# GeGLU block on one core: the plain halves of eight tile pairs first, and M1 held in the memory of h

## The chip, the core and the metric

One of the eight cores of a Trainium2 chip runs the whole program. Its engines work side by side, each in the order of its own instruction stream: TensorE (PE in the profile, with its weight loads as PEld) multiplies matrices into eight banks of accumulator memory of 128 x 512 f32; VectorE (DVE), ScalarE (ACT) and GpSimd (POOL) do the elementwise work; SyncE (SP) issues transfers, and ACT issues some too. The metric is the device time of one launch in microseconds. The median of three runs was 539.03 us before the change (538.69 to 539.42).

## The reference

```python
def reference(x, w_gate, w_up, w_down):
    return (_gelu(x @ w_gate) * (x @ w_up)) @ w_down
```

x is 2,048 tokens by 1,024 (D), the gate and up weights are 1,024 by 3,584 (F), the down weights 3,584 by 1,024, all bf16; gelu is the tanh form. Call h the product of gelu and up, 2,048 by 3,584.

## The kernel before

**Halves and blocks.** The tokens are worked in two halves of 1,024; in each, h is made whole (gate and up) and then multiplied by the down weights. A half has two token blocks of 512 (tb 0 and 1). F is cut into 28 tiles of 128 columns, seven chunks of four tiles; a pair is two tiles. D is cut into eight slices of 128, that is two K halves of four slices.

**Seven products for eight.** For a pair of tiles, two token blocks and two K halves, the plain way takes eight block products of four matmuls each, for gate and again for up: 64 matmuls. The kernel uses a Strassen-Winograd scheme of seven products, 56 matmuls. M1 and M2 are plain (bf16: tile 0 of the pair by block 0, first and second K half), and their sum is tile 0 on block 0. The five others (M5, M6, M7, M3, M4, in this order) multiply sums: s1 to s4 and a copy a22 of the weight blocks of the pair, and t1 to t4 and a copy b22 of the token blocks. The sums are stored as f32r (four bytes) in `s_mem` and `t_mem`, so these are the f32 matmuls of the profile. The t sums are made once per half, by DVE (b22 by ACT). The s sums are made for every pair, eight by POOL (s1, s2, s3, s4 for gate and up, index j) and two copies by ACT; there is one buffer for each, so POOL may overwrite s1 for the next pair once M5 has read it, and so on.

**One group.** `quads` (L406) works two pairs at a time in the eight banks, which are named in twos (one for gate, one for up): PB, VB, QB, RB. M1 goes to a first bank and ACT copies it to Q (L444); M2 is added to the first bank, which ACT (gelu) and DVE (multiply, L291) turn into a tile of h. Then for each pair: M5 into V, copied to memory m by ACT (L472); M6 added to Q, copied to R by ACT (L478); DVE adds m to Q (L434); M7 added to R, DVE writes R + m to V, which gives tile 1 on block 1; M3 added to Q gives tile 0 on block 1; M4 added to R gives tile 1 on block 0. Functions in a dictionary (`thens`) are called at named points between these steps; they place other work in the streams.

**The start.** The first pair of the first half is not done by the scheme: `first_pair_units` (L329) computes it plainly on both blocks, 64 bf16 matmuls (L267), while x and the weights arrive, and the t sums are made (`t_sum`, L241). The first x slices are transposed by TensorE (`transpose_x0`, L302), the others by transposing transfers on SP. Pair 1 then runs alone through `quads`, with sums made early: M5 twice ahead of M6 there, and one quarter of t4 on POOL. Six groups of two pairs follow. In the gaps of these groups DVE makes sums of the down weights, stored to a scratch tensor in device memory (`stage_step`, L614: 42 steps, each a DVE operation, most with a store); `run_steps(n)` places the next n of them, `run_loads` the loads ahead of them and `run_x` transposing transfers of the second half's x.

**Order.** Every helper `pe`, `act`, `dve`, `pool`, `sp` ties an instruction behind the previous one of its engine (`on`, L110): each stream is exactly the order in which the kernel's code calls them. An instruction that waits holds all that stand behind it on its engine. Eight transfer semaphores are used in turn, and a transfer is issued only when the transfer eight places earlier has landed.

**Memory.** The weights of two chunks are held in `w_mem` (`new_chunk`, L146), by even and odd chunk number; hT, 28 rows of 1,024 tokens, is h of one half, with a row for each tile.

Of the kernel before, what the change touches and what calls it, by code (L numbers as in the profile page):

```python
# [10 lines left out]
BF16 = mybir.dt.bfloat16  # L11
# [23 lines left out]
def kernel(  # L35
# [8 lines left out]
    nc = tc.nc  # L44
# [97 lines left out]

    xs0 = w_mem[:, 4 * CH : 4 * CH + TSB * D].rearrange("p (a b) -> p a b", b=D)
    chunks = {}

    def new_chunk(key):  # L146
        c0 = 2 * CH * (key[1] % 2)
        chunks[key] = tuple(
            w_mem[:, c0 + j * CH : c0 + (j + 1) * CH].rearrange(
                "p (a b) -> p a b", b=FG  # L150
            )
            for j in range(2)
        )
# [33 lines left out]
    load_x0(0, sp, 0, 2)  # L187
    load_x0(0, act, 2, TSB)
    load_w(first, 0, 0, 2, sp, 0, FA)
    load_x0(1, act)  # L190
    load_w(first, 1, 0, 2, sp, 0, FA)
    load_w(first, 0, 2, 5, act, 0, FA)
    load_w(first, 1, 2, 5, sp, 0, FA)
# [20 lines left out]
    load_xT(xT, 0, 0, KH, KH + 1)  # L214
    behind_transpose = last_on["sp"]
    load_xT(xT, 0, 0, KH + 1, KH + 2)
    for j in range(2):
        load_w(first, j, 5, KD, act, 0, FA)
        tc.add_manual_dep(
            last_on["act"].ins,  # L220
            behind_transpose.ins.name,
            SCHED_DEP,
            reason="engine order",
        )
    act(nc.scalar.preload_act_table(ACT.Gelu_apprx_tanh))
    load_xT(xT, 0, 0, KH + 2, KD)
    for k0, k1 in ((0, 2), (2, KH), (KH, KD)):
        load_xT(xT, 0, 1, k0, k1)
    for j in range(2):
        load_w(first, j, 0, KD, sp, FA, FG)  # L230
    new_chunk((0, 1))
    for j in range(2):
        load_w((0, 1), j, 0, KD)
# [31 lines left out]
    def mm_gu(ps, w_sb, fi, tb, kd):  # L265
        pe(
            nc.tensor.matmul(  # L267
                ps[:],
                lhsT=w_sb[:, kd, fi * P : (fi + 1) * P],
                rhs=xT[tb][:, kd, :],  # L270
                start=(kd == 0),
                stop=(kd == KD - 1),
            )
        )

# [23 lines left out]
    def unit_out(hT, bset, fi, tb):  # L299
        mult(hT, gelu(banks[bset[0]]), banks[bset[1]], fi, tb)  # L300

    def transpose_x0(q):  # L302

        parts = [(2 * q, 0, 4), (2 * q + 1, 0, 4)]
        if q == 0:
            parts = [(0, 0, 2), (0, 2, 4), (1, 0, 4)]
        for n, (kd, ts0, ts1) in enumerate(parts):
            tp = banks[(PB + QB)[(2 * q + n) % 4]][:].bitcast(BF16)
# [14 lines left out]
    def part(held, tb, k0, k1, us=(0, 1), js=(0, 1)):  # L323
        for kd in range(k0, k1):
            for j in js:
                for u in us:
                    mm_gu(banks[held[u][j]], chunks[first][j], u, tb, kd)

    def first_pair_units(hT):  # L329

        held = (VB, RB)
        transpose_x0(0)
        warm(RB[1], TB // 2)
        part(held, 0, 0, KPQ, js=(0,))
        transpose_x0(1)
        part(held, 0, 0, KPQ, js=(1,))
        part(held, 0, KPQ, KD)
        t_sum("t1", 0, KH // 2)
        t_sum("t1", KH // 2, KH)
        for u in range(2):  # L340
            unit_out(hT, held[u], u, 0)
        held = (QB, PB)
        part(held, 1, 0, KH)
        t_sum("t2")
        t_sum("b22")
        t_sum("t3", 0, KH // 2)
        part(held, 1, KH, KD, (0,))
        unit_out(hT, held[0], 0, 1)
        t_sum("t3", KH // 2, KH)
        part(held, 1, KH, KD, (1,))  # L350
        unit_out(hT, held[1], 1, 1)
        for j in range(2):
            s_sum(0, 1, j, "s3", True, False)
        for name in ("s1", "s2", "s4"):
            for j in range(2):
                s_sum(0, 1, j, name)
# [5 lines left out]
    def block(key, j, i, kh):  # L362
        fi = 2 * (key[2] % PPG) + i
# [704 lines left out]
```

## Time and profile before

| | |
|---|---|
| median of three runs | 539.03 us |
| span of the profiled execution | 537.4 us (its own time lies with the runs, 538.69 to 539.42) |
| TensorE busy | 533.6 us, 2,388 matmuls recorded |
| DVE, ACT, POOL busy | 367.6, 263.5, 252.2 us |
| first plain product (L267) | 4.98 us |
| first product of `quads` | 19.66 us |
| first f32 product | 22.93 us |
| gate and up of the first half end | 182.87 us |
| granted TensorE clock, mean | 1.000 |

How to read it: matmuls are pipelined, so their recorded lengths overlap and the rate is read from starts, or from the length of a run of them. In a timeline a row gives start, length, engine, line, operation, output <- inputs, shapes and how many instructions were merged; in square brackets stands the idle time ahead of it and what ended that. Lengths of DVE and POOL rows overlap by some 0.04 to 0.09 us.

### The profile page before, as it was taken

The page shows a single profiled execution, that of the slowest core. Times are in us where ns is not written, and L with a number is a line of the kernel's source. Part 1 is how long each engine was busy: PE and PEld are TensorE (multiplying, and loading weights), DVE is VectorE, ACT ScalarE, POOL GpSimd, SP SyncE. Part 2 cuts the span into 40 slices and gives each one's busy share as a digit, 9 for nine tenths or more (in the row PEclk, how much of TensorE's full clock was granted, in tenths as well). Part 3 has the DMA queues.
Part 4 walks back from the last instruction along what each step waited for, and adds up shares of the span by engine and source line. Part 5 has one row for each costly group of instructions (what it writes and reads, how often), then busy time and mean ns, then how long its engine had stood idle before and what let it go on. Part 6 is the DMA issues. An engine that isn't in the chain of part 4 may idle for free.

```text
span 537.4 us, 7033 instructions
## 1 busy us (share of the span) xinstructions
PE 533.6 (99%) x2388; PEld 379.2 (71%) x2388; DVE 367.6 (68%) x476; ACT 263.5 (49%) x447; POOL 252.2 (47%) x213
## 2 busy tenths in 40 slices
PE   9999999999999999999999999999999999999997
PEld 4568686867677686777768676776768686866866
DVE  2985868787876998989555353444444669979961
ACT  2555555556465329117465554656555551452280
POOL 0698696969696200000056494958677670000000
PEclk9999999999999999999999999999999999999999
DMA  9965759697623887788950413314040329677846
GB/s 220 329 199 134 267 164 304 182 320 199 229 53 143 318 288 243 243 292 292 329 168 12 145 62 97 110 48 154 3 156 22 136 84 337 228 237 250 292 143 212
DMA packets 92547, 102.70 MB, mean 191 GB/s; under 512 B 18656, under 2 KB 67424, under 8 KB 92512
## 3 DMA queue, kind: packets, MB, share of 16 engines
q1 hardware_dynamic: 69568, 80.23, 45.7%
q10 hardware_dynamic: 22944, 22.02, 13.2%
q8 instruction: 19, 0.31, 0.3%
q14 instruction: 16, 0.13, 0.1%
HBM read 85.98 MB, written 12.58 MB: 183 GB/s over the span
## 4 chain that ended last, share of the span: by engine, by line
PE 99%; ACT 0%; issue 0%
PE bank L418 63%; PE bank L698 33%; PE bank L267 3%; PE bank L202 1%; PE bank L311 0%; ACT o_sb L754 0%
## 5 line engine op out<-in xcount | busy, mean ns | idle before, releaser
L418 PE MATMUL bank<-t_mem,s_mem 128*128 128x512 f32 x1056 | 244.6, 392 | 0.0
L418 PEld LDWEIGHTS bank<-t_mem,s_mem 128*128 128x128 f32 x1056 | 198.1, 188 | 42.7 <-issue 0.2
L388 POOL TENSOR_TENSOR s_mem<-w_mem 128x512 fp32r<-128x512 bf16 x102 | 124.0, 1236 | 185.5 <-DMA out_dram<-o_sb 96.9
L698 PE MATMUL bank<-t_mem,s_mem 128*128 128x512 f32 (+1 forms) x548 | 127.2, 391 | 0.0
L698 PEld LDWEIGHTS bank<-t_mem,s_mem 128*128 128x128 f32 x548 | 102.5, 188 | 22.0
L291 DVE TENSOR_TENSOR hT<-w_mem,bank 128x512 bf16<-128x512 f32 x106 | 72.5, 687 | 66.5 <-PE bank L418 44.5
L434 DVE TENSOR_TENSOR bank<-bank,m 128x512 f32<-128x512 f32 x108 | 70.0, 694 | 56.1 <-ACT m L472 54.3
L418 PE MATMUL bank<-xT,w_mem 128*128 128x512 bf16 x432 | 95.7, 379 | 0.0
L286 ACT ACTIVATE w_mem<-bank 128x512 f32<-128x512 f32 x106 | 63.0, 597 | 64.1 <-DVE bank L434 34.8
L418 PEld LDWEIGHTS <-w_mem 128*128 128x128 bf16 x432 | 41.2, 98 | 51.3 <-issue 3.4
L388 POOL TENSOR_TENSOR s_mem<-w_mem,s_mem 128x512 fp32r<-128x512 bf16 x52 | 68.4, 1335 | 2.9 <-PE bank L418 2.9
L600 DVE TENSOR_TENSOR t_mem<-w_mem 128x1024 fp32r<-128x1024 bf16 x56 | 65.9, 1225 | 0.9 <-PE bank L418 0.9
L388 POOL TENSOR_TENSOR s_mem<-s_mem,w_mem 128x512 fp32r<-128x512 f32 x52 | 61.3, 1200 | 0.0
L401 ACT CAST s_mem<-w_mem 128x512 fp32r<-128x512 bf16 x54 | 33.2, 616 | 31.3 <-PE bank L418 30.1
L478 ACT COPY bank<-bank 128x512 f32<-128x512 f32 x54 | 30.8, 570 | 26.6 <-PE bank L418 26.6
L670 DVE TENSOR_TENSOR s_mem<-hT 128x512 fp32r<-128x512 bf16 x52 | 36.7, 745 | 7.1 <-PE bank L698 7.1
L472 ACT COPY m<-bank 128x512 f32<-128x512 f32 x54 | 31.8, 589 | 18.4 <-PE bank L418 18.4
L698 PEld LDWEIGHTS <-hT 128*128 128x128 bf16 x224 | 21.3, 98 | 26.6 <-issue 2.1
L444 ACT COPY bank<-bank 128x512 f32<-128x512 f32 x54 | 30.7, 570 | 14.3 <-PE bank L418 13.5
L625 DVE TENSOR_TENSOR o_sb<-wd_sb,o_sb 128x512 fp32r<-128x512 bf16 x28 | 32.9, 1176 | 0.5
L763 ACT CAST o_sb<-bank 128x512 bf16<-128x512 f32 x27 | 14.8, 585 | 33.8 <-PE bank L698 33.8
L597 ACT CAST t_mem<-w_mem 128x1024 fp32r<-128x1024 bf16 x28 | 26.9, 1047 | 0.0
(46 smaller groups left out, 236.5 us busy)
## 6 DMA issues: line engine op xcount, KB each, us to landing
t_mem<-t_dram SPq DMA_DIRECT2D x56, 512.0 KB, 5.3
w_mem<-in_w_gate_dram ACTq DMA_DIRECT2D x10, 1024.0 KB, 5.4
w_mem<-in_w_up_dram ACTq DMA_DIRECT2D x10, 1024.0 KB, 8.3
wd_sb<-in_w_down_dram SPq DMA_DIRECT2D x28, 256.0 KB, 5.4
t_dram<-o_sb SPq DMA_DIRECT2D x28, 256.0 KB, 3.5
wd_sb<-in_w_down_dram SPq DMA_DIRECT2D x12, 512.0 KB, 7.6
w_mem<-in_w_down_dram SPq DMA_DIRECT2D x4, 1024.0 KB, 6.7
w_mem<-in_w_down_dram SPq DMA_DIRECT2D x8, 512.0 KB, 8.3
```

What stands on the lines that cost most here:

```text
L286: act(nc.scalar.activation(out=g_sb, in_=ps[:], func=ACT.Gelu_apprx_tanh))
L291: nc.vector.tensor_tensor(out=hT[:, fc, tb * TB : (tb + 1) * TB], in0=g_sb, in1=ps[:], op=ALU.mult,)
L388: pool(nc.gpsimd.tensor_tensor(out=t, in0=in0, in1=in1, op=op))
L401: act(nc.scalar.copy(out=t, in_=a(1, 1)))
L418: nc.tensor.matmul(banks[bank][:], lhsT=lhs[:, c, :], rhs=rhs[:, c, :], start=start and c == 0, stop=c == KH - 1, skip_group_check=True,)
L434: nc.vector.tensor_tensor(out=banks[dst][:], in0=banks[src][:], in1=m5[:], op=ALU.add)
L472: act(nc.scalar.copy(out=m5[j][:], in_=banks[V_[j]][:]))
L478: act(nc.scalar.copy(out=banks[R_[j]][:], in_=banks[Q_[j]][:]))
L600: dve(nc.vector.tensor_tensor(out=t, in0=in0, in1=in1, op=ALU.subtract))
L625: dve(nc.vector.tensor_tensor(out=t, in0=in0, in1=in1, op=ALU.subtract))
L670: dve(nc.vector.tensor_tensor(out=t, in0=in0, in1=in1, op=op))
L698: nc.tensor.matmul(banks[bank][:, c0:c1], lhsT=lhs(i, u), rhs=rhs(i)[:, c0:c1], start=start and i == 0, stop=stop and i == NS - 1, skip_gr ...
```

## The change

- The first half's pairs are formed anew: the first eight pairs are tile p with tile p + 8 (p from 0 to 7), the other six pairs two neighbours as before.
- `first_units` takes the place of `first_pair_units`: it computes tiles 0 to 7 on block 0 alone, plainly, two tiles at a time with gate and up in four banks, two such sets in the eight banks. That is M1 (slices 0 to 3) and M2 (slices 4 to 7) of the eight pairs. Between the two K halves ACT copies M1 of each tile, for gate and for up, as f32 into rows of hT that are not yet written (`p_hold`, `hold`).
- Then `quads` runs with all eight pairs and `plain=False`: no M1 and M2, only the five sums' products of each pair; ACT fetches the held M1 into Q ahead of each pair. In this run s3 of gate is made by DVE, the others by POOL, and M5 stands ahead of M6 in each pair.
- t4 is made by DVE whole; its quarter on POOL is gone. In the stream of DVE t1 stands behind the multiplies of the first two sets, t2 and t3 behind those of the third, then the multiplies of the fourth.
- Loads: x and chunk 0 in other pieces and with the x transposes of four slices in one transfer; chunk 0 (and later chunk 3) lies in hT; chunks 1 and 2 are loaded at the start on SP, chunk 1 ahead of the second block's x, chunk 2 behind it. Chunk 3 is loaded by ACT in two halves, at the start of pairs 1 and 3, chunks 4 and 5 at pairs 4 and 7. The staging loads are moved behind the start.
- One staging step stands at the start and at M3 of pairs 1 to 7; then three groups of two pairs follow, each with four steps at M1, three at the start of the sums, and one at M3 and one at M4 of each pair.

The core of the diff:

```diff
+    NL = 8
+    LEAD = tuple((p, p + NL) for p in range(NL))
+    HF = 2 * NL
+    HELD = ((0, 0), (0, 3))
...
+    def p_hold(pair, j):
+        if j == 1 and pair % 2 == 1:
+            return hT0[:, pair - 1 : pair + 1, TB:SH].bitcast(F32)
+        f = NL + pair if j == 0 else KF - 4 + pair // 2
+        m = hT0[:, f : f + 1, :].rearrange("p a (b c) -> p (a b) c", b=2)
+        return m.bitcast(F32)
...
-    load_xT(xT, 0, 0, KH + 2, KD)
-    for k0, k1 in ((0, 2), (2, KH), (KH, KD)):
+    load_xT(xT, 0, 0, KH, KD)
+    for f0 in (FA, 0):
+        for j in range(2):
+            load_w(first, j, KH, KD, sp, f0, f0 + FA)
+    new_chunk((0, 1))
+    for k0, k1 in ((0, KH), (KH, KD)):
+        for j in range(2):
+            load_w((0, 1), j, k0, k1)
+    for k0, k1 in ((0, KH), (KH, KD)):
         load_xT(xT, 0, 1, k0, k1)
-    for j in range(2):
-        load_w(first, j, 0, KD, sp, FA, FG)
-    new_chunk((0, 1))
-    for j in range(2):
-        load_w((0, 1), j, 0, KD)
+    new_chunk((0, 2))
+    for f0 in (0, FA):
+        for j in range(2):
+            load_w((0, 2), j, 0, KD, sp, f0, f0 + FA)
...
+    def hold(held, tiles, j):
+        for u, t in enumerate(tiles):
+            act(nc.scalar.copy(out=p_hold(t, j), in_=bank2(held[u][j])))
...
+        outs(*rest(1))
+        outs(*rest(0))
+        for j in range(2):
+            top(2, j, 0, KH)
+        for j in range(2):
+            top(3, j, 0, KH)
         t_sum("t1", 0, KH // 2)
         t_sum("t1", KH // 2, KH)
...
+        outs(*rest(2))
         t_sum("t2")
+        t_sum("t3", 0, KH // 2)
+        t_sum("t3", KH // 2, KH)
         t_sum("b22")
...
+        outs(*rest(3))
+        for name in ("s3", "s1", "s2", "s4"):
             for j in range(2):
-                s_sum(0, 1, j, name)
+                s_sum(0, 0, j, name)
...
-    def quads(hT, h, members, nxt, thens, m5_first):
+    def quads(hT, h, members, nxt, thens, m5_first, plain=True):
...
+        def fetch(n):
+            for j in range(2):
+                act(nc.scalar.copy(out=bank2(run[n][4][j]), in_=p_hold(n, j)))
...
+                    dve_too = not plain and (name, j) == ("s3", 0)
+                    s_sum(after[0], after[1], j, name, dve_too, False)
...
+            if not plain and n + 1 < len(run):
+                fetch(n + 1)
...
+            thens[0]["start"] = [
+                lambda j=j: s_sum(0, 0, j, "a22") for j in range(2)
+            ] + [lambda: t_sum("t4", 0, KH // 2)]
+            thens[0]["m5"] = [lambda: t_sum("t4", KH // 2, KH - 1)]
+            thens[0]["v of gate"] = [lambda: t_sum("t4", KH - 1, KH)]
+            for n in range(1, len(LEAD)):
+                thens[n]["start"] = [lambda: run_steps(1), run_loads]
+                thens[n]["m3"] = [lambda: run_steps(1), run_loads]
...
+            thens[1]["start"].append(lambda: load_half(0))
+            thens[3]["start"].append(lambda: load_half(FA))
+            thens[4]["start"].append(lambda: load_chunk((0, 4)))
+            thens[7]["m7"] = [lambda: load_chunk((0, 5))]
+            quads(hT, h, range(len(LEAD)), (h, begin), thens, True, False)
...
-                few = lead == begin
-                add(0, "m1", lambda n=3 if few else 4: run_steps(n))
-                add(0, "start", lambda n=1 if few else 3: run_steps(n))
+                add(0, "m1", lambda: run_steps(4))
+                add(0, "start", lambda: run_steps(3))
...
+                    add(n, "m4", lambda: run_steps(1))
```

## The prediction

> **What bounds the kernel now.** I read the page's busy shares first, then the chain that ended last in order of time, then the timeline of TensorE, and last the timelines of DVE and POOL in the first 40 us, where the change is made.
>
> ```profile
> span 537.4 us, 7033 instructions
> PE 533.6 (99%) x2388; PEld 379.2 (71%) x2388; DVE 367.6 (68%) x476; ACT 263.5 (49%) x447; POOL 252.2 (47%) x213
> PE bank L418 63%; PE bank L698 33%; PE bank L267 3%; PE bank L202 1%; PE bank L311 0%; ACT o_sb L754 0%
> ```
>
> ```profile
> 4.98 1.44 PE bank L267 x4
> ...
> 6.87 12.95 PE bank L267 x60
> 19.82 163.21 PE bank L418 x728
> ```
>
> ```profile
> 39.02 18.51 PE L418 MATMUL bank<-t_mem,s_mem 128*128 128x512 f32 x80
> 57.37 7.08 PE L418 MATMUL bank<-xT,w_mem 128*128 128x512 bf16 x32
> 64.10 18.51 PE L418 MATMUL bank<-t_mem,s_mem 128*128 128x512 f32 x80
> 82.45 7.08 PE L418 MATMUL bank<-xT,w_mem 128*128 128x512 bf16 x32
> ```
>
> ```profile
> 15.24 2.29 DVE L262 TENSOR_TENSOR t_mem<-xT,t_mem 128x2048 fp32r<-128x2048 bf16 x1
> 17.45 2.18 DVE L262 TENSOR_TENSOR t_mem<-xT 128x1024 fp32r<-128x1024 bf16 x1
> ...
> 20.14 1.58 DVE L262 TENSOR_TENSOR t_mem<-xT 128x1024 fp32r<-128x1024 bf16 x1
> 21.64 0.68 DVE L291 TENSOR_TENSOR hT<-w_mem,bank 128x512 bf16<-128x512 f32 x1
> 22.24 2.62 DVE L386 TENSOR_TENSOR s_mem<-w_mem 128x512 fp32r<-128x512 bf16 x2
> ...
> 25.39 1.60 DVE L262 TENSOR_TENSOR t_mem<-xT,t_mem 128x1024 fp32r<-128x1024 bf16 x1
> 26.91 1.95 DVE L434 TENSOR_TENSOR bank<-bank,m 128x512 f32<-128x512 f32 x3
> 28.77 0.93 DVE L262 TENSOR_TENSOR t_mem<-xT,t_mem 128x512 fp32r<-128x512 bf16 x1
> 29.62 0.69 DVE L434 TENSOR_TENSOR bank<-bank,m 128x512 f32<-128x512 f32 x1
> ```
>
> ```profile
> 20.60 3.72 POOL L388 TENSOR_TENSOR s_mem<-s_mem,w_mem 128x512 fp32r<-128x512 f32 x2
> 24.27 3.74 POOL L388 TENSOR_TENSOR s_mem<-w_mem,s_mem 128x512 fp32r<-128x512 bf16 x2
> 27.97 1.17 POOL L260 TENSOR_TENSOR t_mem<-xT,t_mem 128x512 fp32r<-128x512 bf16 x1
> 29.83 2.29 POOL L388 TENSOR_TENSOR s_mem<-w_mem 128x512 fp32r<-128x512 bf16 x2 [0.68 <-PE bank L418]
> ```
>
> TensorE is the chain from 0.77 us to the end and waits for next to nothing. So a matmul less is time won, and any wait that reaches TensorE is time lost. A plain bf16 matmul costs 12.95/60 = 0.216 us. A group of two pairs takes 82.45 - 57.37 = 25.08 us for 32 bf16 and 80 f32 matmuls, so an f32 one costs (25.08 - 32 x 0.216)/80 = 0.227 us, and four of them 0.91 us. The DVE lines are the pass in which the block sums are made for the first pair of sums; the next-to-last block shows that this pass, from t2's start to the add that frees the gate-and-up bank (29.62 + 0.69), lasts 15.06 us with no idle. The POOL lines show one operation at 1.13 to 1.17 us alone, and 1.6 to 2.1 us where DVE runs an operation on memory beside it; DVE's own are stretched too (a half of t3 is 2.18 and 1.58 here, against 1.22 for the same size at 11.64).
>
> **Part 1: matmuls.** The trace has 720 plain bf16 and 1,644 f32 matmuls (80 of the bf16 ones ahead of the first sum); the instructions of the changed program, as built, hold 48 fewer bf16 and 40 more f32: the first pair is no longer computed plainly on both blocks. 48 x 0.216 - 40 x 0.227 = 10.4 - 9.1: **-1.3 us**, all on the path. No row says that these matmuls could have another pace, so both ends are -1.3.
>
> **Part 2: the sums of the token blocks now stand behind the plain halves, with no cover after them.** The first f32 matmul was due at 23.12 (19.66 plus 16 x 0.216) and is due 48 x 0.216 later: 33.5. Call t = 33.5 the start of the sums. Their ten products take 0.91 us each: M5 twice, M6 twice, M7 from t + 3.6, M3 from t + 5.4, M4 from t + 7.3; the last product, M4 of up, is due at 41.6. Before, 3.5 us of plain products stood between the block sums and M5, and the pass began 8 us ahead of it.
> After, DVE's order puts t2 behind the two multiplies of the third set, whose last product ends 16 plain matmuls ahead of t, at 30.0. The multiplies start 0.60 apart (rows of that kind), so t2 starts at 31.2. Until M4 of up, DVE has: t2, t3 in halves, two multiplies, t4's first half, two adds, a quarter of t4, an add, another quarter of t4 (POOL's before), s3 of the next pair (POOL's for most pairs before), an add. All wait only for DVE itself.
> - Lowest: every operation at its undisturbed start-to-start time, 2.2 + 1.26 + 1.15 + 0.6 + 0.6 + 1.15 + 0.6 x 4 + 0.72 + 0.6 + 0.7 = 11.4 us: ready at 42.6, 1.0 us late.
> - Nearest row: the pass shown above, 15.06 us from t2 to the same add. The new one has a multiply (0.65) and an s3 (1.31) less and a quarter of t4 (0.93) more: 14.0 us, ready at 45.2, 3.6 late. But in that pass t2 ran undisturbed at 2.29; POOL is now busy with the first pair's sums in that time, so I add 0.5 (the mean stretch of the six disturbed rows: 0.95, 0.36, 0.36, 0.97, 0.37, 0.25).
> - Highest: each of the seven memory operations waits for most of a POOL operation (0.95, the largest stretch): 11.4 + 6.6 = 18, ready at 49.2, 7.6 late.
> I take **+4.2 us**, by the nearest row. On the way M7 of up waits for a bank that the second of those multiplies holds, M3 for the adds into its banks, M4 for t4's last quarter; these fall inside the 4.2. A rule speaks against the change here. The Trainium skill, SBUF — State Buffer, "two separate sides", says that DVE operations with two inputs in memory and GpSimd operations exclude each other for the whole instruction. The trace agrees in the main: at 34.9 us two such DVE operations take 1.53 us each and POOL's 1.6, against 0.68 and 1.13 alone, nearly the two in turn. By the rule in full the stall would be the upper end, 7.6, and the sum 546.4; by the nearest row it is 543.0.
>
> **Part 3: what must be there by then.** For pair 0 POOL makes eight sums from the weights of chunks 0 and 2; the last piece it needs is behind about 7.0 MB. In the five stretches of 5 us from the start the trace moved 171, 257, 226, 322 and 355 GB/s, and 244 in the next: 7.0 MB at some 26.5 us. Five operations of 1.13 from there bring s2 of up to 32.2; it is due at 36.2. POOL's cover is 4 us; without it each late us is a us. Cost **0** (0 to 2). The second block's transposes pass SP behind chunk 1's loads, about 6 MB: due in front of t1, which has until 33.
>
> **Part 4: the start.** Weights of four tiles, not two, are wanted from 5 us; the first eight loads carry 1.0 MB, as before 1.15. One transpose of four blocks replaces three; a like one landed 4.4 us after its issue at 10.32 (ACT waited for it until 14.8), so issued near 5 it is there at 10, due at 12.8. The weights behind it (rows of 4.6 to 5.7 us to landing, issued at about 7.3) come at 12 to 13. Holding M1 costs 16 copies from a bank on ACT; no row has one into this memory, but the copies to m are 0.59 and from bank to bank 0.57. The fourth pair of copies frees its bank about 0.1 us after it is wanted. **+0.3** (0 to 1.0; a gain is excluded, TensorE had no idle there).
>
> **Part 5: the eight pairs.** 40 x 0.227 = 9.1 us each. POOL has seven sums, 7 x 1.13, and three DVE operations that stretch it by 0.47: 9.3. It falls 0.2 us back in a pair, 1.6 in seven; the sums are finished about 6 us ahead of their use, so **0** (0 to 3, if each stretch is 0.68 or more). DVE has seven bank operations at 0.61 and three others at about 1.2: 7.9. ACT has eleven of 0.57 to 0.62, 6.5, with M1 fetched from memory instead of copied between banks: 0. The loads of chunk 3 now stand on ACT ahead of the M5 copies of pairs 1 and 3, and wait for POOL's last sum that reads the old weights; with two issues (0.4 and 0.5 in the rows) the copies come 1 to 2 us late, of which M7 forgives 0.3 to 1. **+0.4** (0 to 1.8). The other moved issues on SP (staging loads, their stores, next block's x) have a pair's time each: 0.
>
> **Part 6: the staged sums** of the down weights start a pair later and run 11 instead of 9 to a group. In the group at 82.45 DVE is free 0.7 us before the first add; one step more (0.68 to 1.5) fits in front of the multiplies, except in the last group, where two more sums stand there: **+0.4** (0 to 1).
>
> **Sum.** -1.3 + 4.2 + 0 + 0.3 + 0.4 + 0.4 = +4.0. The profiled execution spans 537.4 us; the median of the runs is 539.03, 1.6 us of which lie around the span, so it stands with the other runs. 539.0 + 4.0 = **543.0 us**.
>
> **Rivals.**
> - *The gain is kept.* If DVE has add and s3 behind it at 41.6, the saved matmuls remain: 539.0 - 1.3 = 537.7. It decides if t2 starts before 30.2. For it: every transfer has landed by then and DVE is idle from about 24 us. Against it: the order, in which t2 stands behind those multiplies. Chance 0.06.
> - *Undisturbed DVE:* 539.0 - 1.3 + 1.0 and up to 1.3 from parts 4 to 6: 538.7 to 540.0, about no change (0.2%, 1.1 us, is what a measurement here can tell). Against it: POOL is seldom idle from 27 us on. 0.08.
> - *POOL becomes the bound* of the eight pairs: at 0.9 per stretch, 10.6 us a pair against 9.1, 10.5 in seven less the 6 of lead: about 4.5 more, 547.5. 0.10.
> - *Late weights of chunk 2* (2 us): 545. 0.07.
> - *TensorE's clock falls.* The first matmuls take 0.43 us until 5.8 us, then 0.216. If the gaps in pair 0 bring that back for 3 us, 1.5 us more: 544.5. The Trainium skill, TensorE: Matmul & The Clock Gate, Part 1, asks for an idle window of 3.4 us; my gaps are 2 us at most. 0.03.
> - That the change leaves the matmuls in is excluded by the count in part 1.
>
> **Numbers.** My forecast has 0.66 and runs from 540.5 to 546. Low end of the range 539.7 (cuts off the kept gain and most of the undisturbed case), high end 547 (leaves out most of POOL's). Faster 0.06, same 0.08, slower 0.86.
>
> **What the profile would show.** Right: TensorE at 0.216 to about 33.5 us, then gaps in the first 40 f32 matmuls alone that sum to some 4 us, their releasers DVE (adds, t4) and ACT's copy to the R banks; t2 starting at 31 to 32 us; pairs 2 and 4 to 7 at 9.1 us. Wrong: t2 running before the multiplies, DVE ahead of M4, or TensorE waiting for POOL or for transfers; and then the sum is off by the term of that part.

## The result and the profile after

| | before | after |
|---|---|---|
| median of the runs | 539.1 us (538.69 to 539.42) | 551.74 us (550.42 to 553.68) |
| ratio after to before | | 1.0239, interval 1.0215 to 1.0262 |
| span of the profiled execution | 537.4 us | 549.4 us (its own time 551.18) |
| first f32 product starts | 22.93 us | 36.38 us |
| granted TensorE clock, mean | 1.000 | 0.992 |

The kernel became 12.7 us slower. The forecast was 543.0 us, and its range ended at 547.0: the sign was right and the size was a third of what came. The page after, with its busy times and the chain by engine:

```profile
span 549.4 us, 7112 instructions
PE 536.3 (98%) x2359; PEld 382.6 (70%) x2380; DVE 370.9 (68%) x487; ACT 274.1 (50%) x471; POOL 259.8 (47%) x214
PE 86%; DMA 5%; SPq 4%; DVE 3%; POOL 1%; issue 1%; ACT 0%; ACTq 0%; DVEq 0%; POOLq 0%
```

TensorE was nearly the whole chain before; now 5% of it are transfers, 4% the issues of SP and 3% DVE. The timeline of TensorE tells where (in brackets the idle time ahead of a run of matmuls and what ended it):

```profile
19.32 13.98 PE L337 MATMUL bank<-xT,w_mem 128*128 128x512 bf16 x62
36.38 11.75 PE L470 MATMUL bank<-t_mem,s_mem 128*128 128x512 f32 x36 [3.08 <-POOL s_mem L438]
49.38 4.85 PE L470 MATMUL bank<-t_mem,s_mem 128*128 128x512 f32 x20 [1.26 <-DVE bank L486]
55.71 60.87 PE L470 MATMUL bank<-t_mem,s_mem 128*128 128x512 f32 x264 [1.48 <-ACT bank L531]
...
123.15 18.51 PE L470 MATMUL bank<-t_mem,s_mem 128*128 128x512 f32 x80
...
155.45 12.94 PE L470 MATMUL bank<-t_mem,s_mem 128*128 128x512 f32 x56 [1.40 <-DVE bank L486]
...
190.45 3.89 PE L470 MATMUL bank<-t_mem,s_mem 128*128 128x512 f32 x16 [0.61 <-DVE bank L486]
```

There are five waits: one in front of the first product of sums (for POOL), one in front of M4 of up of pair 0 (49.38, for DVE), one in pair 1 (55.71, for ACT), and two in the groups of two pairs. The first 16 f32 matmuls show something else. Where nothing else holds them their starts lie 0.427 us apart, not 0.227, and the granted clock says the same. The columns are busy time and count of PE, PEld, DVE, ACT and POOL, then the granted clock, the share of the transfer engines and GB/s:

```profile
35.00:40.00 5.00, 3.60 (x8) 2.40 (x9) 5.00 (x5) 0.59 (x1) 5.00 (x4) 0.60 0.44 160
40.00:45.00 5.00, 5.00 (x17) 3.80 (x16) 2.14 (x4) 1.73 (x3) 5.00 (x5) 0.72 0.00 0
```

In the kernel before these two windows have a granted clock of 1.00. The chain between 25 and 60 us joins the events in order (start, duration, what):

```profile
24.25 6.64 DMA w_mem<-in_w_up_dram
...
31.05 5.28 POOL s_mem L438 x2
...
36.38 2.08 PE bank L470 x4
...
46.18 0.97 DVE t_mem L282
47.15 1.57 DVE s_mem L436
48.72 0.62 DVE bank L486
...
49.38 4.85 PE bank L470 x20
```

And two transfers are on the chain in the groups:

```profile
145.66 6.64 DMA t_dram<-o_sb
...
179.16 8.62 DMA w_mem<-in_w_down_dram
```

Set against the kernel before, the profiled span grew by 12.0 us. The sum by stages, in this one execution and from starts of matmuls:

| stage | change |
|---|---|
| 48 bf16 matmuls less, 40 f32 more | -1.3 |
| plain products end at 33.1; by the pace before 22.93 + 48 x 0.216 = 33.3 | -0.2 |
| wait in front of the first f32 product, 33.1 to 36.38 | +3.2 |
| eight pairs, 36.38 to 116.42 = 80.0, for 320 x 0.227 = 72.7 | +7.3 |
| groups, 25.08, 26.73 and 25.96 for 25.08 each | +2.5 |
| down product of the first half and the end | +0.5 |

The 7.3 of the eight pairs are: 14 intervals at 0.427 instead of 0.227, 2.8; the gap of 1.645 us before M4 of up, less one interval, 1.4; the gap of 1.865 in pair 1, 1.6; 0.08 at each of six fetches, 0.5; and short gaps in pair 0, 1.0 (what is left). Pairs 2 to 7 take 9.19 us each.

### The profile page after: what moved, and what is told of

Its sections match the earlier page's. It is cut to its first block, busy times and chain, and to the rows that moved or that the text cites. A ratio compares the mean times of both kernels' runs of the same rounds, so it can differ in the third digit from the quotient of the medians.

```text
span 549.4 us, 7112 instructions
## 1 busy us (share of the span) xinstructions
PE 536.3 (98%) x2359; PEld 382.6 (70%) x2380; DVE 370.9 (68%) x487; ACT 274.1 (50%) x471; POOL 259.8 (47%) x214
## 4 chain that ended last, share of the span: by engine, by line
PE 86%; DMA 5%; SPq 4%; DVE 3%; POOL 1%; issue 1%; ACT 0%; ACTq 0%; DVEq 0%; POOLq 0%
PE bank L470 54%; PE bank L747 32%; SPq L196 2%; DMA w_mem<-in_w_down_dram 2%; DVE o_sb L674 1%; DMA t_dram<-o_sb 1%; DMA w_mem<-in_w_up_dram 1%; SPq L185 1%; POOL s_mem L438 1%; DMA hT<-in_w_up_dram 1%; DVE bank L486 1%; DVE t_mem L649 0%; DVE t_mem L282 0%; DVE s_mem L436 0%; DVE hT L300 0%
## 5 line engine op out<-in xcount | busy, mean ns | idle before, releaser
L470 PE MATMUL bank<-t_mem,s_mem 128*128 128x512 f32 x1096 | 257.4, 395 | 7.8 <-DVE bank L486 3.3
L470 PEld LDWEIGHTS bank<-t_mem,s_mem 128*128 128x128 f32 x1096 | 206.3, 190 | 56.4 <-POOL s_mem L438 4.5
L438 POOL TENSOR_TENSOR s_mem<-w_mem 128x512 fp32r<-128x512 bf16 x83 | 102.5, 1256 | 159.5 <-DVE t_mem L282 97.2
L747 PEld LDWEIGHTS bank<-t_mem,s_mem 128*128 128x128 f32 x548 | 102.3, 188 | 22.5 <-DVE t_mem L649 0.3
L470 PE MATMUL bank<-xT,w_mem 128*128 128x512 bf16 x310 | 70.3, 379 | 0.5
L438 POOL TENSOR_TENSOR s_mem<-w_mem,s_mem 128x512 fp32r<-128x512 bf16 x46 | 59.2, 1307 | 3.4 <-PE bank L470 3.4
L470 PEld LDWEIGHTS <-w_mem 128*128 128x128 bf16 x320 | 30.5, 98 | 38.0 <-issue 2.6
L438 POOL TENSOR_TENSOR s_mem<-s_mem,w_mem 128x512 fp32r<-128x512 f32 x46 | 53.4, 1183 | 0.0
L531 ACT COPY bank<-bank 128x512 f32<-128x512 f32 x56 | 31.9, 571 | 25.1 <-PE bank L470 25.1
L451 ACT CAST s_mem<-w_mem 128x512 fp32r<-128x512 bf16 x48 | 29.5, 617 | 25.7 <-PE bank L470 24.5
L496 ACT COPY bank<-bank 128x512 f32<-128x512 f32 x40 | 22.8, 570 | 10.4 <-PE bank L470 10.4
L674 DVE TENSOR_TENSOR o_sb<-wd_sb,o_sb 128x512 fp32r<-128x512 bf16 x28 | 25.1, 898 | 0.4
```

The source lines that it names most:

```text
L438: pool(nc.gpsimd.tensor_tensor(out=t, in0=in0, in1=in1, op=op))
L451: act(nc.scalar.copy(out=t, in_=a(1, 1)))
L470: nc.tensor.matmul(banks[bank][:], lhsT=lhs[:, c, :], rhs=rhs[:, c, :], start=start and c == 0, stop=c == KH - 1, skip_group_check=True,)
L531: act(nc.scalar.copy(out=banks[R_[j]][:], in_=banks[Q_[j]][:]))
L674: dve(nc.vector.tensor_tensor(out=t, in0=in0, in1=in1, op=ALU.subtract))
L747: nc.tensor.matmul(banks[bank][:, c0:c1], lhsT=lhs(i, u), rhs=rhs(i)[:, c0:c1], start=start and i == 0, stop=stop and i == NS - 1, skip_gr ...
```

## The experiments

All are edits of the kernel after, unless another is named. They were compared with runs of the kernel before on the same chip (539.1 to 539.5 us). Gaps between matmuls are given from start to start. Times of the start-up transfers differ by 0.5 to 1 us from one execution to the next, so single times below 1 us there are not read. "M4 of up" is its first matmul in pair 0.

The start of the products of sums differs by more. `e3_steps` and `e4_half_late`, two of the runs below, have the code of the kernel after up to pair 1, and yet started them earlier than 36.38 us, first `e3_steps`, then `e4_half_late`:

```profile
34.84 1.20 PE L470 MATMUL bank<-t_mem,s_mem 128*128 128x512 f32 x4 [1.27 <-POOL s_mem L438]
```

```profile
35.84 1.94 PE L470 MATMUL bank<-t_mem,s_mem 128*128 128x512 f32 x4 [1.93 <-POOL s_mem L438]
```

They stood 1.4 and 2.1 us behind the end of the plain products, against 3.2 in the kernel after. So the table above holds for one execution, and a gain of up to 1.5 us at the start is not by itself the work of an edit.

### Why does POOL start late?

POOL waited until 29.27 us for weights of chunk 2. The timeline of SP shows that they were issued behind the two transposing transfers of the second token block, in whose issue SP stood for 9.87 us:

```profile
13.71 9.87 SPq L196 DMA_TRANSPOSE xT<-in_x_dram  x2
23.62 0.58 SPq L185 DMA_DIRECT2D w_mem<-in_w_gate_dram  x1
24.25 0.95 SPq L185 DMA_DIRECT2D w_mem<-in_w_up_dram  x1
```

**Chunk 2's first halves ahead of the transposing transfers** (`e1_c2_ahead`).

```diff
-    for k0, k1 in ((0, KH), (KH, KD)):
-        load_xT(xT, 0, 1, k0, k1)
     new_chunk((0, 2))
-    for f0 in (0, FA):
-        for j in range(2):
-            load_w((0, 2), j, 0, KD, sp, f0, f0 + FA)
+    for j in range(2):
+        load_w((0, 2), j, 0, KD, sp, 0, FA)
+    for k0, k1 in ((0, KH), (KH, KD)):
+        load_xT(xT, 0, 1, k0, k1)
+    for j in range(2):
+        load_w((0, 2), j, 0, KD, sp, FA, FG)
```

> Changed kernel with one edit: on SP the first halves of chunk 2 (gate and up) are issued ahead of the two transposes of the second block's x, not behind them. Theory Q (queue): pair 0's weights came at 30.9 us because SP stood 7.8 us in the first of these transposes and could issue them only at 23.6; so POOL starts by about 22 to 25 us (29.3 before the edit), the first f32 matmul at about 33.0 (36.4), with no half-rate matmuls behind it; the DVE pass then shows as the stall of pair 0, M4 of up at 45 to 46.5 us (49.4), in all 3 to 4.5 us less: 547 to 549 us. Rival B (bytes): it is the 7 MB ahead of them that take the time whatever the order; POOL starts after 28 us and the time stays within 1 us of 551.7.

Measured: 548.82 us, ratio 1.0171 (1.0154 to 1.0188). POOL starts at 24.30 and the f32 products at 33.53 without the long gap. But x comes later now: t1 starts at 27.61 instead of 23.86 and t2 at 32.47 instead of 30.94, DVE and POOL are stretched against each other, and M4 of up starts at 49.55, in the place where it was (49.38). Gaps of 1.71, 1.53 and 2.18 us in pair 0 have taken the place of the one before it, and eight matmuls between 42.0 and 45.5 us run at half rate. So late weights alone do not set the end of pair 0. Of the 2.9 us won, 1.6 are pair 1's wait, which is gone (a gap of 0.31 there).

**The same bytes without transposing** (`e11_plain_x`). The transposing transfers are replaced by plain ones, so the second token block holds weights instead of x.

```diff
     for k0, k1 in ((0, KH), (KH, KD)):
-        load_xT(xT, 0, 1, k0, k1)
+        sp(nc.sync.dma_start(out=xT[1][:, k0:k1, :], in_=wgv[:, k0:k1, 0:TB]))
```

> The two transposing transfers that bring the second token block of x (1.05 MB) are replaced by plain transfers of as many bytes from w_gate, so the second token block holds weights instead of x; nothing else is changed. Theory X (a transposing transfer and plain transfers in flight shut each other out, on whatever queue): SP is through with these issues before 17 us instead of 23.6, chunk 2's first halves land before 27 us, POOL starts by 27.5, TensorE's f32 products start at 33.3 without the 3.5 us gap and at the full rate; the time falls by 5 to 8 us, to 544 to 547. Theory Y (it is the bytes: what must land before pair 0 is more than the transfers bring): chunk 2 lands at 28.5 or later, the gap stays over 2 us and the time within 2 us of 551.7.

Measured: 549.20 us, ratio 1.0191 (1.0174 to 1.0208). What the transfers moved in two stretches, first in the kernel after, then here (last column, GB/s):

```profile
15.00:20.00 5.00, 5.00 (x25) 2.28 (x24) 1.92 (x4) 1.30 (x3) 0.00 (x0) 1.00 1.23 347
20.00:25.00 5.00, 4.95 (x24) 2.29 (x24) 1.78 (x3) 2.66 (x6) 0.00 (x0) 1.00 1.14 159
```

```profile
15.00:20.00 5.00, 5.00 (x25) 2.25 (x23) 2.27 (x4) 1.08 (x2) 0.00 (x0) 1.00 1.08 354
20.00:25.00 5.00, 4.95 (x23) 2.24 (x23) 1.90 (x3) 3.01 (x6) 0.00 (x0) 1.00 1.13 322
```

From 20 to 25 us the transposing transfers cost (322 - 159) x 5 = 0.8 MB, 2.5 us at 322 GB/s, and POOL's first two sums start that much earlier:

```profile
26.81 1.16 POOL L438 TENSOR_TENSOR s_mem<-hT,w_mem 128x512 fp32r<-128x512 bf16 x1 [25.51 <-DMA w_mem<-in_w_gate_dram]
28.57 1.15 POOL L438 TENSOR_TENSOR s_mem<-hT,w_mem 128x512 fp32r<-128x512 bf16 x1 [0.60 <-DMA w_mem<-in_w_up_dram]
```

SP was through with these two issues at 16.45 us, and the f32 products ran from 32.60 with 0.36 us lost ahead of the second one, at the full rate at first: that part of theory X holds. Its time does not: M4 of up still starts only at 46.92, 5.3 us behind its due time of 41.6, after gaps of 1.29, 1.30, 0.94 and 2.17 us, and seven matmuls then run at half rate. DVE had no idle from t2 at 30.59 to the last add at 46.86: this pass of 16.3 us sets M4 of up here. A wait in the groups also grew, to 2.51 us idle ahead of 154.12 (1.40 in the kernel after), with seven matmuls at half rate behind it, which takes back some of the time. About 2.5 us of the late landing came from transposing; the landing at 28.6 is what is left without it.

### Is the half rate a cost of its own?

**Fifteen matmuls that nobody reads, in the first wait** (`e2_dummies`).

```diff
             first_units(hT)
+            for _ in range(15):
+                warm(PB[0])
```

> Changed kernel with one edit: 15 matmuls of constants (128x512 bf16, 0.216 us each) stand behind the plain products, ahead of the first f32 matmul, in the bank that M5 of gate clears afterwards. They fill the wait of 3.4 us. Theory C (clock): the matmuls from 36.4 to 42.9 us ran at 0.427 us because TensorE had stood still for 3.4 us; so with the dummies all f32 matmuls start 0.227 apart at once, and pair 0 ends 2 to 3.4 us earlier: 548.3 to 549.8 us. Rival S (sums): the 0.427 us is the speed at which weights or token sums arrive beside the busy DVE and POOL; then the spacing stays 0.43 and the time 551.7.

Measured: 551.09 us, ratio 1.0216 (1.0201 to 1.0232). The timeline of TensorE and two windows of this kernel:

```profile
33.21 3.44 PE L227 MATMUL bank<-const-bfloat16-1.0 128*128 128x512 bf16 x15
36.30 2.19 PE L470 MATMUL bank<-t_mem,s_mem 128*128 128x512 f32 x8
39.29 7.01 PE L470 MATMUL bank<-t_mem,s_mem 128*128 128x512 f32 x28 [0.80 <-POOL s_mem L438]
47.97 4.83 PE L470 MATMUL bank<-t_mem,s_mem 128*128 128x512 f32 x20 [1.67 <-DVE bank L486]
55.39 6.91 PE L470 MATMUL bank<-t_mem,s_mem 128*128 128x512 f32 x22 [2.60 <-ACT bank L531]
```

```profile
35.00:40.00 5.00, 4.20 (x19) 2.69 (x18) 5.00 (x5) 1.17 (x2) 5.00 (x4) 1.00 0.37 134
...
55.00:60.00 5.00, 4.61 (x13) 3.70 (x14) 4.21 (x6) 2.54 (x6) 3.91 (x5) 0.66 0.45 128
```

The products start at 36.30 and run at the full rate beside busy DVE and POOL, which goes against rival S. How much the dummies won cannot be read from this run. POOL had s1 of gate, which the first product waits for, ready at 35.03 us here (31.83 + 3.20), so the dummies, which end at about 36.3, held the start themselves. And `e3_steps`, without dummies, also ran at the full rate and reached M4 of up at 47.72 (47.97 here, 49.38 in the kernel after). What ties the half rate to idleness is the record of the clock in all runs together (last section). Pair 1 then reaches ACT's loads earlier, waits 2.99 us instead of 1.87, and eight matmuls behind that gap run at half rate. The time is the same within 0.7 us: one loss hides another.

### The two causes behind pair 0

**Chunk 3's loads at M7 instead of the start of pairs 1 and 3** (`e4_half_late`). ACT issued them ahead of the M5 copies and stood there until POOL had read the old weights.

```diff
-            thens[1]["start"].append(lambda: load_half(0))
-            thens[3]["start"].append(lambda: load_half(FA))
+            thens[1]["m7"] = [lambda: load_half(0)]
+            thens[3]["m7"] = [lambda: load_half(FA)]
```

> Changed kernel with one edit: the loads of chunk 3 on ACT are issued behind M7 of pairs 1 and 3, not ahead of their M5 copies. Theory A: the gap of 1.9 us in pair 1 is ACT standing at these issues until POOL has read the old weights (the second was issued at 53.6, the copies of M5 only then); so the gap goes, M7 of pair 1 follows at once: 1.5 us less, 550.1 to 550.4 us. Rival P: the copies would have come late anyway, since the bank for M5's copy or POOL's sums are late in pair 1; the gap stays at over 1 us and the time at 551.2 to 551.7.

Measured: 547.87 us, ratio 1.0185 (1.0139 to 1.0231; three runs at 547.6 to 548.0, one at 552.36). Pair 1's gap is gone, as theory A has it (49 matmuls in a row behind M4 of up, at 48.72), and the eight pairs take 78.3 us. That gap was worth 1.6 us; the median fell by 3.9. Some of the rest lies ahead of the edit, which stands in pair 1: in the profiled execution M4 of up came 0.7 us earlier, with half as many matmuls at half rate. Where all of it came from is open.

**The staging steps at M4 moved from the groups to pairs 3 to 7** (`e3_steps`).

```diff
+            for n in range(3, NL):
+                thens[n]["m4"] = [lambda: run_steps(1)]
...
-                    add(n, "m4", lambda: run_steps(1))
```

> Changed kernel with one edit: the staged sum at M4 of each pair of the three groups is taken away (4, 3 and 1 per pair: 9 to a group, as before the change) and five are put at M4 of pairs 3 to 7. Theory G (bursts): the gaps of 1.8 us at 153.7 and 1.0 us at 189.5 come from eight sums in a row with four buffers that must be stored first, and from the sums that stand ahead of the adds in the last group; so the three groups take 25.1 us each (25.1, 26.7 and 26.0 before the edit), 2 to 2.5 us less: 549.3 to 549.8 us, if pairs 3 to 7 stay at 9.2 us. Rival D: DVE has no room in the eight pairs (7.9 of 9.1 us busy by the prediction), and they lose what the groups win: 551 to 552 us.

Measured: 550.03 us, ratio 1.0193 (1.0173 to 1.0214). The groups take 25.41, 25.08 and 25.08 us, so 2.2 of their 2.5 us were the steps at M4. But the eight pairs end 1.0 us later than in the kernel after: they started 1.5 us earlier (34.84) and at the full rate, with the same code up to there, and lost more than that to a wait of 3.00 us in pair 1 and eight half-rate matmuls behind it. So of the 2.2 us only 1.7 are left in the time.

### The order of DVE, and all together

**t2 and t3 directly behind t1** (`e5_sums_first`), ahead of the multiplies of the third set.

```diff
-        outs(*rest(2))
         t_sum("t2")
         t_sum("t3", 0, KH // 2)
         t_sum("t3", KH // 2, KH)
+        outs(*rest(2))
         t_sum("b22")
```

> t2 and t3 move directly behind t1, ahead of the multiplies of the third set. Theory P (the first pair's stall is set by VectorE's sums of token blocks, in one place, whatever the weights do): M4 of up starts about 2 us earlier than 49.4, the gap of 1.6 us before it goes, and the time falls by 1.5 to 2 us, to about 549.5. Theory Q (the late weights of chunk 2 on GpSimd set it, the sums only follow): TensorE still starts its f32 products at about 36.4 after the gap of 3.5 us and at half rate, M4 of up comes where it was, and the time stays within 0.5 us of 551.7.

Measured: 547.52 us, ratio 1.0148 (1.0131 to 1.0165), 4.2 us less; neither theory had more than 2. M4 of up comes at 47.22, as theory P has it, but the gap in front of it did not go: it is 2.18 us, and eight matmuls behind it run at half rate. POOL still starts at 29.46, and yet the f32 products are at the full rate from 35.19, after a gap of 1.67 us instead of 3.46. With t2 done at 29.9 DVE is off POOL's way sooner: from the start of POOL's second sum to the end of s1 of gate, its third, it takes 3.9 us, against 5.3 in the kernel after and 4.3 in `e2_dummies`, `e3_steps` and `e4_half_late`. In the other three of the four runs the granted clock was 1.000 throughout; in the sixteen runs of the kernel after, `e1_c2_ahead`, `e3_steps` and `e4_half_late` it was so once.

**The same, with chunk 2's first halves on ACT's queue** (`e6_both`), past the transposing transfers.

```diff
+    def late_loads():
+        for j in range(2):
+            load_w((0, 2), j, 0, KD, act, 0, FA)
+        for k0, k1 in ((0, KH), (KH, KD)):
+            load_xT(xT, 0, 1, k0, k1)
...
         top(1, 1, KPQ, KH)
+        late_loads()
```

> As e5_sums_first, and chunk 2's first halves are issued on ScalarE's queue at about 14 us, past SP's transposing transfers, which keep their place. Together the two causes of pair 0's stalls are gone if theories P and Q both hold: f32 products from about 33.3 us at the full rate, no gap over 0.6 us before M4 of up, and a time lower by 3.4 (wait) + 2.8 (clock) + 1.6 (M4 of up) = 7.8 us, about 544; pair 1's wait for chunk 3's loads (1.9 us) and the groups' 2.5 us stay. If what e1_c2_ahead showed is instead a limit of transfers (the loads now take the rate from the x block), f32 still starts before 34.5 but t1 and t2 come later by 1 us or more and the time stays above 547.

Measured: 552.59 us, ratio 1.0247 (1.0219 to 1.0275). Timelines of SP, POOL and DVE of this kernel:

```profile
15.96 14.19 SPq L196 DMA_TRANSPOSE xT<-in_x_dram  x2
```

```profile
29.13 1.16 POOL L442 TENSOR_TENSOR s_mem<-hT,w_mem 128x512 fp32r<-128x512 bf16 x1 [27.83 <-DMA w_mem<-in_w_gate_dram]
```

```profile
30.68 3.32 DVE L285 TENSOR_TENSOR t_mem<-xT,xT 128x1024 fp32r<-128x1024 bf16 x2 [7.13 <-DMA xT<-in_x_dram]
```

ACT issued the two loads at 16.92 and 19.94 us, and still they landed no earlier than in the kernel after (29.13 against 29.27), while the transposing transfers took 14.2 us instead of 9.9 and t1 started 6.8 us later. This agrees with the second branch of what was expected. The next two kernels have the same loads, and in one of them the weights of gate did land earlier (`e7_all`; in `e8_all_t4` POOL starts at 29.61):

```profile
25.45 1.15 POOL L442 TENSOR_TENSOR s_mem<-hT,w_mem 128x512 fp32r<-128x512 bf16 x1 [24.15 <-DMA w_mem<-in_w_gate_dram]
```

In all three t1 started late, at 28.96 to 30.86 instead of 23.86. So another queue brings the weights forward at times, and x back each time. Since t2 and t3 now stand ahead of the multiplies, TensorE waits 6.82 us at M5 of up for a bank that those multiplies free. The same order that won 4 us with x in time loses with x late.

**This with both edits behind pair 0,** those of `e3_steps` and `e4_half_late` (`e7_all`).

> As e6_both, with chunk 3's loads at M7 of pairs 1 and 3 (e4_half_late) and the sums' steps ahead of the groups (e3_steps). If the four causes add up: 551.7 - 7.8 - 1.8 - 2.5 = 539.6, within 0.6 of the kernel before. If they hide one another (a wait taken away uncovers the next, as in e2_dummies), it stays above 542.

Measured: 550.49 us, ratio 1.0204 (1.0186 to 1.0222): the groups are at 25.1 to 25.3 us, but the gap at M5 of up is 7.56 us.

**And with t4 beside the fourth set's multiplies, s3 of pair 1 on POOL, M6 ahead of M5 from pair 1 on** (`e8_all_t4`; the loads of `e6_both` as well):

```diff
-        outs(*rest(3))
+        held3 = rest(3)
+        t_sum("t4", 0, KH // 2)
+        outs(*held3)
+        t_sum("t4", KH // 2, KH)
...
-                    dve_too = not plain and (name, j) == ("s3", 0)
+                    dve_too = not plain and (name, j) == ("s3", 0) and n > 0
...
-            ] + [lambda: t_sum("t4", 0, KH // 2)]
-            thens[0]["m5"] = [lambda: t_sum("t4", KH // 2, KH - 1)]
-            thens[0]["v of gate"] = [lambda: t_sum("t4", KH - 1, KH)]
+            ]
...
-            if not plain:
+            if not plain and n == 0:
                 order = (do_m5, 0), (do_m5, 1), (do_m6, 0), (do_m6, 1)
```

> As e7_all, and what VectorE does in pairs 0 and 1 is lightened: t4 is made beside the multiplies of the fourth set instead of inside pair 0, pair 1's S3 of gate is made by GpSimd, and M6 keeps its place behind M4 in the pairs from 1 on. If VectorE's queue is the last cause in pair 0, the lead takes 73.5 us at most and the time is 537.5 to 539.0, up to 1.5 us under the kernel before (the change's matmuls are worth 1.3). If t4 in front of pair 0's adds only moves the wait to its first M4, the time is that of e7_all or up to 2 us above it.

Measured: 548.93 us, ratio 1.0177 (1.0162 to 1.0192). The eight pairs take 80.3 us, with gaps of 3.25 us (for POOL) and 3.02 us (for the multiplies) and sixteen half-rate matmuls (four and twelve); x was late again, t1 at 30.86. `e6_both`, `e7_all` and `e8_all_t4` rest on a wrong idea of the transfers, and say little on the rest.

**Without the detour of the loads** (`e9_four`): t2 and t3 first, both edits behind pair 0, and s3 of pair 1 on POOL; the loads as in the kernel after.

```diff
-        outs(*rest(2))
         t_sum("t2")
...
+        outs(*rest(2))
...
-                    dve_too = not plain and (name, j) == ("s3", 0)
+                    dve_too = not plain and (name, j) == ("s3", 0) and n > 0
...
+            for n in range(3, NL):
+                thens[n]["m4"] = [lambda: run_steps(1)]
...
+            thens[1]["m7"] = [lambda: load_half(0)]
+            thens[3]["m7"] = [lambda: load_half(FA)]
```

> e5_sums_first with the groups' steps ahead (e3_steps), chunk 3's loads at M7 (e4_half_late) and pair 1's S3 of gate on GpSimd. From e5_sums_first's 547.5: the groups' gaps 0.57 + 1.79 go, and of the 2.2 us gap in front of M4 of up (S3 of gate, 1.65 us, stands there on VectorE) and the half rate behind it (7 matmuls, 1.4 us) most. That gives 547.5 - 2.4 - 3.0 = 542.1, in 541 to 544. If GpSimd, which is already late with chunk 2, becomes the wait instead, pair 1 shows a gap over 1.5 us and the time stays above 543.5.

Measured: 543.89 us, ratio 1.0101 (1.0076 to 1.0126; three runs at 543.7 to 544.0, one at 546.72). TensorE's timeline and the mean clock of this kernel:

```profile
27.71 6.21 PE L337 MATMUL bank<-xT,w_mem 128*128 128x512 bf16 x27
34.62 2.31 PE L470 MATMUL bank<-t_mem,s_mem 128*128 128x512 f32 x8 [0.70 <-POOL s_mem L438]
37.84 22.35 PE L470 MATMUL bank<-t_mem,s_mem 128*128 128x512 f32 x92 [0.91 <-POOL s_mem L438]
```

```profile
core 0: 542.2 us, clock 1.000
```

The weights are as late as ever (POOL from 29.17), and still 7.9 of the 12.7 us are gone. No gap in pairs 0 and 1 is over 1.3 us and no matmul behind the first sum runs at half rate, in any of the four runs. POOL's sums show why the first product is 1.8 us earlier with the same landing; first the kernel after, then this one:

```profile
31.05 3.18 POOL L438 TENSOR_TENSOR s_mem<-hT,w_mem 128x512 fp32r<-128x512 bf16 x1 [0.62 <-DMA w_mem<-in_w_up_dram]
34.19 4.23 POOL L438 TENSOR_TENSOR s_mem<-w_mem 128x512 fp32r<-128x512 bf16 x2
```

```profile
29.17 4.28 POOL L438 TENSOR_TENSOR s_mem<-hT,w_mem 128x512 fp32r<-128x512 bf16 x2 [27.87 <-DMA w_mem<-in_w_gate_dram]
33.41 2.27 POOL L438 TENSOR_TENSOR s_mem<-w_mem 128x512 fp32r<-128x512 bf16 x2
```

The two sums s1, for the first of which the first product waits, take 2.27 us when t3 is through at 32.4, and 4.23 beside t3 (DVE 33.14 to 37.4); the second sum took 3.18 beside t2. From the start of the second sum to the end of s1 of gate it is 3.3 us here, against 5.3 in the kernel after. Against the three executions with 4.3 us named above, the new order is worth 1 us here; against that of the kernel after, 2.

**And chunk 2 in quarters** (`e10_pieces`), so that pair 0's tiles land without pair 1's.

```diff
-    for f0 in (0, FA):
+    for f0, f1 in ((0, P), (P, FA), (FA, FG)):
         for j in range(2):
-            load_w((0, 2), j, 0, KD, sp, f0, f0 + FA)
+            load_w((0, 2), j, 0, KD, sp, f0, f1)
```

> e9_four with chunk 2's first halves in quarters, so that pair 0's two tiles land without pair 1's. If the bytes behind the transposing transfers set the landing, GpSimd starts 1 to 1.5 us earlier and the f32 products too, 0.8 to 1.3 us off the time of e9_four. If short rows (256 B instead of 512 B) cost as much as they save, the time is that of e9_four within 0.5.

Measured: 544.19 us, ratio 1.0103 (1.0082 to 1.0125), the same as without. POOL starts at 28.03 and the products at 33.77, but its own sums for M6 and M7 stay the limit (a gap of 1.30 at 36.8), and the spread of its runs, 543.05 to 545.64, is wider than the gain looked for, as is that of `e9_four`. So whether quarters help is not decided.

No version ran faster than the kernel before. What remains in the best one: 1.3 us in front of the f32 products (34.62 for 33.3), 4.4 in the eight pairs (77.1 for 72.7), 0.6 in the first group, less 1.3 for the matmuls: 5.0, where 4.8 was measured.

## Why the prediction was wrong in size

- **Part 1** (-1.3) was right: 48 and 40 matmuls, and 9.19 us a pair where nothing waits, 0.08 of it at the fetch.
- **Part 2** named the right work in the right order: t2 started at 30.94, forecast 31.2. Its size was too small. With the weights earlier (`e11_plain_x`) the pass lasts 16.3 us without idle, where 14.0 and 0.5 were forecast, and M4 of up is 5.3 us behind its due time, not 4.2, inside the stated 1.0 to 7.6. In the kernel after this is not a term by itself: from t2 to the last add DVE took 18.4 us, 2.9 of them waiting for banks of a TensorE that was late and slow. The 15.5 that are left compare with 14.0 forecast.
- **Part 3 is the step that failed:** "Cost 0 (0 to 2)". It measured 3.2 us, and 1.4 and 2.1 us in `e3_steps` and `e4_half_late`, which have the same start. By the forecast's numbers (five operations from 26.5 us bring the sixth sum) s1 of gate, the third sum, was ready at 26.5 + 2 x 1.13 = 28.8, 4.5 us ahead of its use at 33.3; it was ready at 36.3. The last piece landed 4.5 us late, at 31.0, and the two operations behind it took 5.3 us for 2.3 (4.3 in three other executions). Of the late landing 2.5 us is the transposing (`e11_plain_x`), to which the forecast gave no price. Another 1.3 us is a unit: the pieces up to there are 7,168 KB of 1,024 bytes, which is 7.34 MB and not 7.0, and by the rates used that is 27.8 us. The 0.7 that are left fit with this, that a rate says when bytes move and a sum can start only once a whole piece has landed. The operations at "1.13" ran beside DVE's t2 and t3 at 1.16 to 3.2 us, which the same text had used against DVE in part 2 and left out for POOL. Where parts 2 and 3 meet, at M4 of up, the forecast was 4.2 us late; it was 7.8, and 6.1 to 7.1 in `e2_dummies`, `e3_steps` and `e4_half_late`.
- **The clock rival** was given 0.03 because "my gaps are 2 us at most". The 3.46 us gap of part 3 broke that, and 2.8 us at half rate followed; and gaps near 2 us were no safety either (last section). The rival of late weights was priced at 2 us, 545, without what its own gap would do to the clock; the two belong in one case.
- **Part 4** said +0.3 and excluded a gain; it was -0.2 in this execution, and 0.1 and 0.4 in `e3_steps` and `e4_half_late`: right within what the start varies.
- **Part 5** had the mechanism on ACT: loads ahead of M5's copies, held by POOL. It cost 1.6 us, not 0.4, all in pair 1 and near its upper end of 1.8; in `e2_dummies` and `e3_steps`, which came to pair 1 earlier, it cost 2.8 and a further 1.6 at half rate. POOL as the bound of the eight pairs did not come true.
- **Part 6** said 0.4 and at most 1; it was 2.5. Moving the M4 steps took 2.2 of it away (`e3_steps`). The row read there showed DVE free for 0.7 us in front of an add; that a sum of down weights can also wait for its store or its load (145.66 and 179.16 in the chain) was not looked at.

These terms are not independent. An earlier pair 0 uncovered pair 1's wait (`e2_dummies`, `e3_steps`); freeing pair 1 left a group gap that moved from one group to the next. A sum of gaps in one execution is what the time is made of, but not what each repair brings: the repairs of four causes in `e9_four`, worth 7.9 us together, are 4.2, 3.9 and 1.7 us where they were tried alone, 9.8 in sum. What the start of an execution happens to do is in each of these figures: of the 3.9, 1.6 are the repair's own. The fourth, s3 on POOL, was not tried alone.

Left open: how much of pair 0's remaining 2 to 3 us belongs to POOL's sums and how much to DVE's. In `e9_four` POOL is busy throughout from 29.17 to 50 us, which speaks for POOL, but no run took sums away from it.

## What to carry to other kernels

Work that is taken out of a pipeline's start also takes the cover from whatever was made beside it: ask for each input of the first uncovered step when its last piece lands, what stands in front of its issue on the queue, and how long its making takes with both DVE and POOL at work. Price a wait on TensorE together with the slower matmuls that may follow it, as one case. When several causes show, repair them together before judging any, and expect the next in line to take up much of a single repair.

## What the hardware showed that was not expected

- **Transposing transfers and plain ones get in each other's way, on both queues tried.** Around 20 us the rate in single slices of half a microsecond fell from 361 to 9 GB/s (in `e6_both` from 311 to 22), and the stretch from 20 to 25 us moved 159 GB/s, against 322 with plain transfers of the same size. SP's issue of two of them took 9.9 us, 14.2 to 16.1 us in three kernels where ACT issued plain loads meanwhile, against 2.16 us for two plain ones. Why the rate falls, no run shows.
- **Half rate came after shorter gaps than thought, and goes by fixed stretches of 3.41 us.** The traces record when the granted clock changes. From one change to the next it is a whole multiple of 3.41 us in every trace here: 9 to 157 times at full rate, one to three times at half rate. So the half rate starts at the end of such a stretch, not when TensorE falls idle. The stretches of the kernel after around its first wait (columns as above: TensorE's busy time and count come first, the granted clock third from the end):

```profile
32.55:35.96 3.41, 0.70 (x3) 0.14 (x2) 3.41 (x3) 1.99 (x4) 3.41 (x2) 1.00 1.07 366
35.96:39.38 3.42, 2.98 (x6) 1.97 (x7) 3.42 (x4) 0.59 (x1) 3.42 (x3) 0.50 0.35 126
39.38:42.79 3.41, 3.41 (x9) 2.59 (x9) 1.24 (x1) 1.03 (x2) 3.41 (x4) 0.50 0.00 0
42.79:46.20 3.41, 3.41 (x16) 2.63 (x16) 2.72 (x5) 0.70 (x2) 3.41 (x3) 1.00 0.00 0
```

And those around the gap of 2.18 us in `e5_sums_first`:

```profile
43.90:47.31 3.41, 1.73 (x8) 0.96 (x6) 3.31 (x5) 3.14 (x6) 3.41 (x3) 1.00 0.01 2
47.31:50.73 3.42, 3.42 (x8) 2.67 (x9) 2.63 (x4) 0.62 (x1) 3.42 (x4) 0.50 0.00 0
```

What decides, as far as these traces show, is how busy TensorE was in one stretch at full rate. In the traces of all these kernels, the clock fell behind each of the nine stretches with 0.27 to 1.44 us busy, and behind none with 1.84 us or more. With 1.73 and 1.74 us, about half of the stretch, it fell twice and stayed twice. So a gap of some 2.1 us can bring the half rate if it lies in one stretch, and did not where an end of a stretch divided it (2.18 us in `e1_c2_ahead`, 2.09 in `e7_all`); where the ends lie differs from one execution to the next. The Trainium skill, TensorE: Matmul & The Clock Gate, Part 1, gives an idle window of about 3.4 us that runs freely. The traces agree with its length and its running freely, but the window need not be idle as a whole: 1.44 us of matmuls in it did not keep the rate. A gap under that window is not safe.
